# A new order of 375 steps for the opening of a fused retention and two-FFN kernel, with the rows of its loads made 8 KB long

## The chip, the cores and the metric

One core of one Trainium2 chip runs the whole program. The metric is the time of one execution on the device in microseconds (us). A core has five engines that run side by side and meet at semaphores: PE (TensorE, matrix products), DVE (VectorE), ACT (ScalarE), POOL (GpSimd) and SP (SyncE), which here only issues DMAs. 16 DMA engines move data between the HBM and the on-chip memory.

## What is computed

A retention layer (attention with a decay in place of a softmax) on 4 x 8 heads, 576 positions of 64 numbers each, and two feed-forward layers over the 2304 tokens of 512 numbers that come out of it, all in float32:

```python
def _attn_ref(q, k, v):
    scores = scale * np.matmul(q, k.transpose(0, 1, 3, 2))
    Dmat = np.where(rel >= 0, gamma[:, None, None] ** rel[None, :, :], 0.0)
    ret = scores * Dmat[None, :, :, :]
    return np.matmul(ret, v)

def reference(**kwargs):
    x = attn_out.transpose(0, 2, 1, 3).reshape(B * S, H * D)
    x = moe_w_out(leaky(x @ moe_w_in))       # leaky(h) = max(0.01 h, h), 512 -> 2048 -> 512
    h = x @ moe2_w_in                        # 512 -> 2048
    return (h * np.cos(h)) @ moe2_w_out      # 2048 -> 512
```

The inputs w_in and w_out come as 64-bit floats, so the kernel loads their raw words and turns them into float32 itself.

## The kernel before

**Tiles.** The 2304 tokens are cut into 18 chunks of 128 tokens (`ch`, four arrays q, k, k, v of 128 x 512, 1 MB a chunk) and into five blocks of the first feed-forward layer, the first of 512 tokens, which is chunks 0 to 3. The weights of that layer are 16 tiles (f = 0 to 15), each a 1 MB raw tile of 128 x 1024 64-bit words; tiles 0 and 15 are loaded as two halves (`raw0a`, `raw0b`), which belong to w_in and w_out.

**The opening.** All code before the second token block is an order written out by hand, the string `FIRST`: 375 names of steps, played from left to right. Each step puts its instructions on one or more engines, and every engine runs its own instructions strictly in the order in which they were put there. For a chunk i the steps are: `ch` load, `sq` and `sv` scale q and v (DVE; `sv` of some chunks is eight instructions on ACT), `s` scores on PE (16 small matrix products), `m` mask on DVE, `v` values and `g` growth of the state (16 products each), `st.0`, `st.1` state sums on DVE, `r.0` and `r` reads of the state on PE, `tk` the result's move to `xr` on ACT. `xh` and `xl` split that result into a high and a low part (ACT, then DVE). `V` is the whole PE part of a chunk of the second block. For a weight tile f the steps are `raw` load, `abs` and `lo` (ACT), `cs` (two DVE instructions), `or`, `add` (DVE), `hi` (ACT) and `low` (DVE): some 5.5 us of DVE a tile. `H f.k` and `O f` are the products of the first and the second half of the layer with that tile (12 products each), `lk`, `gh` (ACT) and `gl` (DVE) lie between H and O. `~n` are products on constants that nobody reads, n blocks of 128 columns.

**What holds a load back.** All loads go through SP, one after the other. Two of them wait on purpose for PE (`in_turn`): the second half of weight tile 0 and tile 1 wait for the scores of a chunk, tiles 2 and 3 for the growth of chunk 3 (`last_of["grown"]`). What follows in SP's order waits behind them.

**After the opening** a planner's list, `SECOND`, orders the rest: four more token blocks of the first layer, the conversion of the second layer's weights (`mraw`, `more`, in 64 loads of 256 KB), and the second layer. It is the same list in both kernels.

A product of 64 x 64 or 128 x 512 in float32 appears in the trace as two weight loads and two matmuls (four instructions); those of H and O as one of each.

Of the kernel before, what the change touches and what calls it, by code (L numbers as in the profile page):

```python
# [50 lines left out]


FIRST = """
ch0 sq0 s0 sv0 m0 raw0a abs0a cs0a or0a ~3 v0 g0 st0.0 st0.1 ~4 r0.0 ch1 sq1 s1 r0 lo0a add0a ch2 m1 sq2 sv1
hi0a low0a v1 g1 s2 st1.0 st1.1 r1.0 sv2 m2 v2 r1 ch3 sq3 sv3 raw0b raw1 tk0 g2 st2.0 st2.1 s3 m3 abs0b tk1
cs0b or0b lo0b add0b r2.0 r2 v3 g3 st3.0 st3.1 ~5 r3.0 r3 abs1 cs1 or1 lo1 hi0b low0b add1 tk2 tk3 xh0 xl0 xh1
xl1 ch4 sq4 xh2 xl2 xh3 xl3 hi1 low1 raw2 raw3 abs2 cs2 ~13 H0.0 H0.1 H0.2 H0.3 H1.0 H1.1 H1.2 H1.3 lk0 gh0
gl0 lo2 abs3 or2 add2 lk1 gh1 O0 gl1 O1 cs3 hi2 low2 H2.0 H2.1 H2.2 H2.3 sv4 V3 raw4 lo3 or3 add3 abs4 cs4 hi3
low3 raw5 raw7 raw6 raw8 ch5 raw9 raw15a or4 lk2 gh2 gl2 lo4 add4 abs5 cs5 H3.0 H3.1 H3.2 H3.3 O2 hi4 lk3 low4
H4.0 H4.1 H4.2 H4.3 gh3 gl3 O3 lo5 or5 add5 abs6 cs6 hi5 lk4 gh4 low5 H5.0 H5.1 H5.2 H5.3 gl4 O4 lo7 lo6 abs7  # L60
or6 add6 cs7 hi6 low6 lk5 gh5 gl5 or7 add7 H6.0 H6.1 H6.2 H6.3 O5 abs8 cs8 hi7 lk6 low7 H7.0 H7.1 H7.2 gh6 gl6
st4.0 or8 lo8 add8 st4.1 raw10 lo10 sq5 raw11 H7.3 lk7 gh7 gl7 m4 O6 O7 hi8 low8 H8.0 H8.1 abs9 abs10 lo9 sv5
cs9 or9 add9 raw12 cs10 hi9 low9 H8.2 H8.3 V4 ch6 or10 lk8 gh8 st5.0 gl8 st5.1 add10 abs11 cs11 H9.0 H9.1 H9.2
H9.3 lk9 gh9 gl9 O8 O9 or11 tk4 hi10 low10 H10.0 H10.1 H10.2 H10.3 raw15b raw13 lo11 add11 raw14 sv6 sq6 m5 V5
ch7 abs12 hi11 lk10 gh10 cs12 low11 gl10 or12 lo12 add12 lo13 abs13 H11.0 H11.1 H11.2 H11.3 lk11 gh11 hi12 sv7
lo14 cs13 gl11 st6.0 m6 st6.1 sq7 O10 O11 tk5 low12 H12.0 or13 add13 hi13 H12.1 H12.2 H12.3 lk12 gh12 abs14
low13 abs15a gl12 V6 st7.0 st7.1 cs14 or14 H13.0 H13.1 H13.2 H13.3 add14 lk13 gh13 gl13 O12 O13 cs15a hi14
low14 or15a abs15b tk6 lo15b cs15b ch8 H14.0 H14.1 H14.2 H14.3 sq8 sv8 lo15a m7 add15a hi15a low15a V7 st8.0
lk14 gh14 gl14 st8.1 tk7 H15.0 H15.1 H15.2 H15.3 O14 lk15 or15b add15b gh15 gl15 hi15b low15b O15 m8 ch9 sq9
sv9  # L70
"""


# [1534 lines left out]
```

## Time and profile before

| what | value |
|---|---|
| median of 3 runs | 822.32 us (821.81 to 822.36) |
| the profiled execution's own time | 823.17 us |
| its span, first to last instruction | 821.0 us, so 2.2 us lie around it |
| PE busy | 805.4 us (98%) |
| DVE, ACT busy | 645.6 us (79%), 539.5 us (66%) |
| DMA | 203.79 MB, mean 248 GB/s |

The busy shares are means over stages with different limits. The opening, which the change is about, is the first 131 us; in it DVE and PE are both nearly full, and what counts is which of them waits for which, and where.

### The profile page before, as it was taken

Reading aid. Unit: us, or ns where it says so; the run is one execution under the profiler, and the core shown is the slowest. Engines: PE = TensorE matmul, PEld = TensorE weight load, DVE = VectorE, ACT = ScalarE, POOL = GpSimd, SP = SyncE. Lnnn points to the kernel's source line nnn. Section 1 sums busy time; section 2 is a strip of 40 time slices with the busy share of each in tenths; the row PEclk is TensorE's granted clock in tenths of the full one; section 3 lists DMA queues with packets and bytes.
Section 4 is the critical chain, followed back from the end, with each engine's and each line's share of the span. In section 5 each row is a group of like instructions: output and inputs, shape, how many; then the busy total and the mean of one; then the engine's idle time right before and its main releaser. Section 6 shows DMA issues by size and latency. Waiting matters only on the chain.

```text
span 821.0 us, 16054 instructions
## 1 busy us (share of the span) xinstructions
PE 805.4 (98%) x6134; PEld 739.5 (90%) x6134; DVE 645.6 (79%) x1148; ACT 539.5 (66%) x1041; POOL 6.6 (1%) x8
## 2 busy tenths in 40 slices
PE   7899999999999999999999999999999999999997
PEld 4578887888888888999999999999999999999997
DVE  5899988888886868786841278789889788788886
ACT  4788866655655455555542399887868868678761
POOL 0000011000000000000000000000000000000000
PEclk9999999999999999999999999999999999999999
DMA  9774615877878868777579286999748997719544
GB/s 324 274 267 154 231 53 191 263 232 240 270 237 263 261 188 284 243 256 221 193 252 395 109 321 248 338 318 377 279 157 308 306 378 275 261 42 383 199 172 162
DMA packets 101309, 203.79 MB, mean 248 GB/s; under 512 B 9072, under 2 KB 54896, under 8 KB 96112
## 3 DMA queue, kind: packets, MB, share of 16 engines
q1 hardware_dynamic: 101088, 202.41, 70.2%
...
## 4 chain that ended last, share of the span: by engine, by line
PE 82%; DVE 8%; DMA 4%; issue 3%; ACT 2%; SPq 0%; DVEq 0%; POOLq 0%; ACTq 0%
PE psum L1263 21%; PE psum L1435 20%; PE psum L616 19%; PE psum L630 19%; DMA ch<-in_qkv 3%; DMA raw<-in_w 1%; DVE t L569 1%; PE psum L401 1%; DVE t L576 1%; DVE w L588 1%; PE psum L464 1%; PE psum L425 1%; DVE t L560 1%; PE psum L363 1%; DVE acc L1472 0%
## 5 line engine op out<-in xcount | busy, mean ns | idle before, releaser
L616 PE MATMUL psum<-x_sb,w 128*128 128x512 f32 (+1 forms) x960 | 212.4, 370 | 2.7 <-DVE x_sb L852 1.3
L630 PE MATMUL psum<-g,w 128*128 128x512 f32 (+1 forms) x960 | 211.5, 370 | 0.0
L616 PEld LDWEIGHTS psum<-x_sb,w 128*128 128x128 f32 x960 | 174.7, 188 | 28.4 <-DVE x_sb L852 2.2
L630 PEld LDWEIGHTS psum<-g,w 128*128 128x128 f32 x960 | 174.3, 188 | 24.6 <-DVE g L651 1.3
L1263 PE MATMUL psum<-x,ws 128*128 128x384 f32 x576 | 111.2, 334 | 1.0 <-ACT psum L1396 1.0
L1263 PEld LDWEIGHTS psum<-x,ws 128*128 128x128 f32 x576 | 100.7, 188 | 1.5 <-ACT psum L1396 1.4
L917 DVE TENSOR_TENSOR g<-graw,g 128x512 fp32r<-128x512 f32 (+1 forms) x64 | 39.8, 623 | 62.2 <-ACT g L914 62.0
L1263 PE MATMUL psum<-x,wa 128*128 128x384 f32 x432 | 83.9, 334 | 0.0
L1435 PE MATMUL psum<-g,wp 128*128 128x384 f32 x432 | 81.7, 335 | 0.8 <-DVE acc L1472 0.7
L1435 PE MATMUL psum<-g,wq 128*128 128x384 f32 x432 | 80.2, 334 | 0.0
L1435 PEld LDWEIGHTS psum<-g,wp 128*128 128x128 f32 x432 | 75.3, 188 | 1.5 <-DVE acc L1472 1.1
L1263 PEld LDWEIGHTS psum<-x,wa 128*128 128x128 f32 x432 | 75.7, 188 | 0.0
L910 ACT ACTIVATE graw<-psum 128x512 f32<-128x512 f32 (+1 forms) x64 | 34.7, 543 | 62.3 <-PE psum L616 62.2
L1435 PEld LDWEIGHTS psum<-g,wq 128*128 128x128 f32 x432 | 75.4, 188 | 0.0
L914 ACT CAST g<-graw 128x512 fp32r<-128x512 f32 (+1 forms) x64 | 36.3, 567 | 49.5 <-PE psum L630 47.9
L1472 DVE TENSOR_TENSOR acc<-psum,acc 128x384 f32<-128x384 f32 x90 | 48.3, 553 | 18.8 <-PE psum L1435 18.4
L1312 DVE SCALAR_TENSOR_TENSOR r<-r,h 128x768 f32<-128x768 int32 x48 | 45.5, 954 | 6.8 <-ACT r L1307 6.4
L1321 DVE SCALAR_TENSOR_TENSOR h<-r,h 128x768 f32<-128x768 f32 x48 | 45.4, 953 | 5.3 <-ACT r L1318 5.1
L1317 ACT ACTIVATE r<-r 128x768 f32<-128x768 f32 x48 | 40.6, 847 | 9.6 <-DVE r L1312 9.4
L1334 DVE TENSOR_TENSOR g<-tq,g 128x768 fp32r<-128x768 f32 x48 | 45.4, 952 | 1.5 <-ACT g L1338 1.4
L1338 ACT CAST g<-tq 128x768 fp32r<-128x768 f32 x48 | 39.6, 837 | 9.9 <-DVE tq L1355 6.2
L1307 ACT CAST r<-h 128x768 int32<-128x768 f32 x48 | 40.1, 838 | 5.8 <-DVE h L1293 3.6
...
## 6 DMA issues: line engine op xcount, KB each, us to landing
ws<-ws SPq DMA_DIRECT2D x20, 1024.0 KB, 8.2
wp<-wp SPq DMA_DIRECT2D x20, 1024.0 KB, 7.4
ch<-in_qkv SPq DMA_DIRECT2D x17, 1024.0 KB, 6.9
...
raw<-in_w SPq DMA_DIRECT2D x14, 1024.0 KB, 10.4
...
```

The source lines that it names most:

```text
L616: nc.tensor.matmul(hp, wt[:, i, cols], x_t[lj, k][:, j, :n], start=(k == 0 and a == 0), stop=(k == KK - 1 and a == 2),)
L630: nc.tensor.matmul(psum[:, BANK_O + m, :n], wt[:, i, cols], gt[:, j, :n], start=(f == 0 and a == 0), stop=(f == NF - 1 and a == 2),)
L917: nc.vector.tensor_tensor(out=g.ap[:, 1, :n], in0=y.ap[:, :n], in1=g.ap[:, 0, :n].bitcast(F32), op=ALU.subtract)
L1263: nc.tensor.matmul(bank[BANKS[m]].rearrange("p (q t) -> p q t", t=Q), a[:, hl, i, j * P : (j + 1) * P], x[:, :, v, j, :], start=m in (1, 5 ...
L1307: "ACT", 885, lambda: nc.scalar.copy(rb.ap.bitcast(I32), pair()),
L1312: nc.vector.scalar_tensor_tensor(out=rb.ap, in0=rb.ap.bitcast(I32), scalar=-1.0, in1=pair(), op0=ALU.mult, op1=ALU.add)
L1317: t = add("ACT", 885, lambda: nc.scalar.activation(rb.ap, rb.ap, AF.Sin, scale=PI), [t], due)
L1321: nc.vector.scalar_tensor_tensor(out=pair(), in0=rb.ap, scalar=0.5, in1=pair(), op0=ALU.subtract, op1=ALU.mult)
L1334: nc.vector.tensor_tensor(out=gb.ap[:, :, 1], in0=src(), in1=gb.ap[:, :, 0].bitcast(F32), op=ALU.subtract)
L1338: h_ = add("ACT", 885 if n == 2 else 515, lambda: nc.scalar.copy(gb.ap[:, :, 0], src()), [*needs, opened["all"]], due, 0, gb.old)
L1435: nc.tensor.matmul(to, wt[:, hl, i, t * P : (t + 1) * P], gt[:, fi, v, :], start=m in (1, 5) and h == 0 and x == 0, stop=h == 1 and x == 2 ...
L1472: x = add("DVE", 560, lambda: nc.vector.tensor_tensor(out=kept(), in0=to, in1=kept(), op=ALU.add), [got], due - SOON / 2)
```

## The change

It replaces the string `FIRST` by another order of the same 375 steps, moves one gate (the second half of tile 0 and tile 1 now wait for the scores of chunk 2, not of chunk 1), and lays the inputs out in the HBM so that a chunk's or a tile's row in one partition is one piece of 8 KB (4 KB for a half tile) where it was four pieces of 2 KB. The 256 KB loads of the second layer's weights keep pieces of 2 KB, which now lie 8 KB apart and not back to back.

```diff
 FIRST = """
-ch0 sq0 s0 sv0 m0 raw0a abs0a cs0a or0a ~3 v0 g0 st0.0 st0.1 ~4 r0.0 ch1 sq1 s1 r0 lo0a add0a ch2 m1 sq2 sv1
...
+ch0 sq0 s0 sv0 m0 ~1 v0 g0 ch1 sq1 s1 ch2 raw0a st0.0 st0.1 m1 sq2 r0.0 r0 sv1 v1 g1 s2 st1.0 st1.1 m2 r1.0 r1
...
-            got = nc.sync.dma_start(ch, qkv[i].rearrange("x p d -> p x d"))
+            got = nc.sync.dma_start(ch, qkv[i])
...
-        return nc.sync.dma_start(raw.rearrange("p (c t) -> p c t", c=4), w[0, f].rearrange("c p t -> p c t"))
+        return nc.sync.dma_start(raw, w[0, f])
...
             if n == 1 or n == 0 and half:
-                in_turn(got, last_of["scores", 1])
+                in_turn(got, last_of["scores", 2])
...
-                nc.sync.dma_start(rb.ap.bitcast(I64), w[1, f, c])
+                nc.sync.dma_start(rb.ap.bitcast(I64), w[1, f, :, c * 2 * P : (c + 1) * 2 * P])
...
-    arrays = {"in_qkv": np.ascontiguousarray(np.stack(parts, axis=1))}
+    arrays = {"in_qkv": np.ascontiguousarray(np.stack(parts, axis=2))}
...
-        layers.append(np.concatenate([w_in, w_out], axis=2).reshape(NF, P, 4, 2 * P).transpose(0, 2, 1, 3))
+        layers.append(np.concatenate([w_in, w_out], axis=2))
```

The three excerpts below show in which order instructions now stand. The first is SP from the program's start, before (L304, L305 and L307 load chunks, L539 a half tile, L534 a whole tile; PE in the brackets is the gate):

```order
1 L304 DMA ch<-in_qkv 128x2x512
2 L305 DMA ch<-in_qkv 128x2x512
3 L539 DMA raw<-in_w 128x2x256
4 L307 DMA ch<-in_qkv 128x4x512 x3
5 L539 DMA raw<-in_w 128x2x256 [waits PE_49]
6 L534 DMA raw<-in_w 128x4x256 [waits DMAHW0_49]
7 L307 DMA ch<-in_qkv 128x4x512 [waits DMAHW1_49,DMAHW2_49,DVE_49,PE_49]
8 L534 DMA raw<-in_w 128x4x256
9 L534 DMA raw<-in_w 128x4x256 [waits DMAHW3_49]
```

and SP from the start in the changed kernel:

```order
1 L304 DMA ch<-in_qkv 128x1024
2 L305 DMA ch<-in_qkv 128x1024
3 L307 DMA ch<-in_qkv 128x2048 x2
4 L539 DMA raw<-in_w 128x512
5 L307 DMA ch<-in_qkv 128x2048
6 L539 DMA raw<-in_w 128x512 [waits PE_49]
7 L534 DMA raw<-in_w 128x1024 [waits DMAHW0_49]
8 L534 DMA raw<-in_w 128x1024 [waits DMAHW1_49,PE_49]
9 L534 DMA raw<-in_w 128x1024 [waits DMAHW2_49]
```

Chunks 1 and 2 now stand ahead of the first half tile, and behind the growth of chunk 3 come two weight tiles (3, then 2) where chunk 4 came first. Next, PE from the start up to the scores of chunk 2, before (L516 and L522 are products on constants, L363 scores, L401 values, L425 growth, L464 reads):

```order
1 L516 MATMUL psum<-zero 128x512 x3
2 L363 MATMUL psum<-ch 64x64 x16
3 L522 MATMUL psum<-tabs_sb,still 128x384
4 L401 MATMUL psum<-p_sb,ch 64x64 x16
5 L425 MATMUL psum<-ch 64x64 x16
6 L522 MATMUL psum<-tabs_sb,still 128x512
7 L464 MATMUL psum<-ch,st 64x64 x4
8 L363 MATMUL psum<-ch 64x64 x16
9 L464 MATMUL psum<-ch,st 64x64 x4
10 L401 MATMUL psum<-p_sb,ch 64x64 x16
11 L425 MATMUL psum<-ch 64x64 x16
12 L363 MATMUL psum<-ch 64x64 x16
```

and the same stretch of PE in the changed kernel:

```order
1 L516 MATMUL psum<-zero 128x512 x3
2 L363 MATMUL psum<-ch 64x64 x16
3 L522 MATMUL psum<-tabs_sb,still 128x128
4 L401 MATMUL psum<-p_sb,ch 64x64 x16
5 L425 MATMUL psum<-ch 64x64 x16
6 L363 MATMUL psum<-ch 64x64 x16
7 L464 MATMUL psum<-ch,st 64x64 x8
8 L401 MATMUL psum<-p_sb,ch 64x64 x16
9 L425 MATMUL psum<-ch 64x64 x16
10 L363 MATMUL psum<-ch 64x64 x16
```

Before the scores of chunk 2 there stand 109 products before the change and 108 after it. Last, PE from H of tile 2 on, before (L616 is H, L630 is O, w_589 tile 2, w_645 tile 3, w_698 tile 4; L425 and L363 in between are V3, the growth and scores of chunk 4):

```order
30 L616 MATMUL psum<-x_sb,w_589 128x512 x12
31 L425 MATMUL psum<-ch 64x64 x8
32 L363 MATMUL psum<-ch 64x64 x16
33 L616 MATMUL psum<-x_sb,w_645 128x512 x12
34 L630 MATMUL psum<-g,w_589 128x512 x12
35 L616 MATMUL psum<-x_sb,w_698 128x512 x12
```

and there in the changed kernel (L614 is H, L628 O; w_605 is tile 3, w_705 tile 5, w_721 tile 6, w_818 tile 7):

```order
28 L614 MATMUL psum<-x_sb,w_605 128x512 x12
29 L628 MATMUL psum<-g,w_595 128x512 x12
30 L614 MATMUL psum<-x_sb,w_665 128x512 x12
31 L628 MATMUL psum<-g,w_605 128x512 x12
32 L614 MATMUL psum<-x_sb,w_705 128x512 x12
33 L628 MATMUL psum<-g,w_665 128x512 x12
34 L628 MATMUL psum<-g,w_705 128x512 x12
35 L614 MATMUL psum<-x_sb,w_721 128x512 x12
36 L425 MATMUL psum<-ch 64x64 x8
37 L363 MATMUL psum<-ch 64x64 x16
38 L614 MATMUL psum<-x_sb,w_818 128x512 x12
```

V3 has moved from behind H of tile 2 to behind H of tile 6. On DVE the scaling of chunk 4's q (`sq4`) has moved in the same way, from ahead of tile 1's last instruction to behind tile 6's `add`.

## Rows read from the trace of the kernel before

**Rows 1.** The page's chain of work that ended last: shares of the span.

```profile
PE 82%; DVE 8%; DMA 4%; issue 3%; ACT 2%; SPq 0%; DVEq 0%; POOLq 0%; ACTq 0%
```

**Rows 2.** Waits of PE from 48 to 145 us: total, times, longest, us.

```profile
PE psum L616 <- DVE x_sb L852: 1.3, 2, 0.9
```

**Rows 3.** Chain of work that ended last, first 120 us: start, us, what.

```profile
19.43 2.31 issue
...
48.00 2.82 PE psum L616 x11
```

**Rows 4.** DVE in order of time, 17 to 50 us: start, us; brackets: idle before.

```profile
22.49 0.69 DVE L384 TENSOR_TENSOR p_sb<-psum,tabs_sb 128x512 f32<-128x512 f32 x1 [2.15 <-PE psum L363]
23.10 0.42 DVE L560 TENSOR_SCALAR t<-t 128x512 f32<-128x512 f32 x1
...
25.45 0.95 DVE L449 TENSOR_TENSOR st<-psum,st 128x256 f32<-128x256 f32 x2
...
31.84 0.69 DVE L315 TENSOR_TENSOR ch<-ch,tabs_sb 128x512 f32<-128x512 f32 x1
32.44 1.29 DVE L604 TENSOR_TENSOR x_sb<-xr,x_sb 128x512 fp32r<-128x512 f32 x2
...
35.40 0.70 DVE L560 TENSOR_SCALAR t<-t 128x1024 f32<-128x1024 f32 x1 [0.53 <-ACT t L552]
```

**Rows 5.** All engines in order of time, 45 to 137 us.

```profile
46.35 0.51 PE L425 MATMUL psum<-ch 64*64 64x64 f32 x10
...
47.43 3.40 PE L616 MATMUL psum<-x_sb,w 128*128 128x512 f32 x12
...
68.70 1.22 DVE L588 TENSOR_TENSOR w<-t,w 128x1024 fp32r<-128x1024 f32 x1
...
69.92 2.91 PE L616 MATMUL psum<-x_sb,w 128*128 128x512 f32 x12
```

**Rows 6.** Landings, seen by who waits for them, in order of time, 0 to 60 us.

```profile
7.24 0.69 DVE L327 TENSOR_TENSOR ch<-ch,tabs_sb 128x512 f32<-128x512 f32 x1 [0.60 <-DMA ch<-in_qkv]
...
11.35 2.02 ACT L322 ACTIVATE ch<-ch,tabs_sb 128x64 f32<-128x64 f32 x8 [1.50 <-DMA ch<-in_qkv]
...
15.07 0.69 DVE L315 TENSOR_TENSOR ch<-ch,tabs_sb 128x512 f32<-128x512 f32 x1 [1.18 <-DMA ch<-in_qkv]
```

**Rows 7.** Stretches: length, busy by engine (x instructions), clock, DMA share, GB/s.

```profile
40.00:46.00 6.00, 5.95 (x26) 4.54 (x25) 5.83 (x7) 5.48 (x12) 0.00 (x0) 1.00 1.05 385
...
750.00:758.00 8.00, 8.00 (x48) 8.00 (x47) 5.75 (x8) 6.83 (x13) 0.00 (x0) 1.00 1.01 409
```

**Rows 8.** PE in order of time, around three places of the opening.

```profile
15.81 1.13 PE L363 MATMUL psum<-ch 64*64 64x64 f32 x32
...
21.74 0.63 PE L363 MATMUL psum<-ch 64*64 64x64 f32 x27 [2.31 <-issue]
...
25.75 0.49 PE L522 MATMUL psum<-tabs_sb,still 128*128 128x128 f32 x2 [0.29 <-issue]
```

**Rows 9.** Stretches from the start: PE and PEld are the first two (x instructions).

```profile
0.00:19.43 19.43, 15.81 (x348) 9.82 (x348) 10.78 (x21) 8.79 (x26) 0.20 (x4) 0.91 0.93 335
...
0.00:25.70 25.70, 19.36 (x476) 12.25 (x476) 14.59 (x28) 12.91 (x34) 0.20 (x4) 0.93 0.74 262
```

**Rows 10.** Instruction queue, 0.1 us from 12.85, 19.25, 22.85, 31.2: packets, MB, share.

```profile
q8 instruction: 1, 0.02, 70.0%
...
q8 instruction: 1, 0.02, 62.5%
...
q8 instruction: 1, 0.02, 89.7%
...
q8 instruction: 1, 0.02, 54.9%
```

**Rows 11.** One raw tile's load, issued at 62.0 us alone: KB, us to landing.

```profile
raw<-in_w SPq DMA_DIRECT2D x1, 1024.0 KB, 5.0
```

**Rows 12.** The stretch with the low clock, columns as in rows 7.

```profile
14.32:17.73 3.41, 3.08 (x108) 2.71 (x99) 2.56 (x5) 2.66 (x11) 0.00 (x0) 0.50 1.04 372
```

More of the change, by code (lines that the diff above doesn't have):

```diff
@@ L53 @@
 FIRST = """
-ch0 sq0 s0 sv0 m0 raw0a abs0a cs0a or0a ~3 v0 g0 st0.0 st0.1 ~4 r0.0 ch1 sq1 s1 r0 lo0a add0a ch2 m1 sq2 sv1
[L55 to L68, printed above, removed]
@@ L69 @@
-lk14 gh14 gl14 st8.1 tk7 H15.0 H15.1 H15.2 H15.3 O14 lk15 or15b add15b gh15 gl15 hi15b low15b O15 m8 ch9 sq9
-sv9
+ch0 sq0 s0 sv0 m0 ~1 v0 g0 ch1 sq1 s1 ch2 raw0a st0.0 st0.1 m1 sq2 r0.0 r0 sv1 v1 g1 s2 st1.0 st1.1 m2 r1.0 r1
+tk0 abs0a cs0a or0a lo0a add0a ch3 sq3 sv3 sv2 hi0a low0a raw0b raw1 ~8 s3 m3 abs0b cs0b v2 g2 st2.0 st2.1 tk1
+lo0b or0b add0b v3 g3 r2.0 r2 st3.0 st3.1 abs1 lo1 cs1 or1 add1 ~2 r3.0 r3 tk2 tk3 xh0 xl0 xh1 xl1 ~12 H0.0
+H0.1 xh2 xl2 raw3 raw2 raw5 raw4 raw6 raw15a ch4 hi0b low0b xh3 xl3 hi1 low1 abs2 cs2 H0.2 H0.3 H1.0 H1.1 lk0
@@ new lines @@
+gh0 gl0 or2 lo2 abs3 add2 H1.2 H1.3 lk1 gh1 gl1 O0 O1 cs3 hi2 low2 lo3 or3 add3 abs4 cs4 hi3 low3 or4 H2.0
+H2.1 H2.2 H2.3 lk2 ~2 H3.0 H3.1 H3.2 H3.3 gh2 gl2 O2 lo4 add4 raw7 raw8 raw9 ch5 abs5 cs5 hi4 lk3 low4 H4.0
+H4.1 H4.2 H4.3 gh3 gl3 O3 or5 lo5 add5 abs6 lo7 cs6 hi5 low5 or6 lk4 lo6 add6 gh4 gl4 sq4 abs7 raw10 hi6 low6
+H5.0 H5.1 H5.2 H5.3 O4 lk5 gh5 gl5 O5 H6.0 H6.1 H6.2 H6.3 cs7 or7 add7 abs8 cs8 sv4 V3 lo8 hi7 low7 or8 lk6
+gh6 gl6 add8 abs9 cs9 H7.0 H7.1 H7.2 H7.3 raw11 O6 hi8 low8 lk7 gh7 gl7 O7 H8.0 H8.1 H8.2 H8.3 raw15b raw12
@@ new lines @@
+lo9 abs10 or9 add9 lo10 hi9 sv5 sq5 st4.0 st4.1 m4 V4 ch6 low9 cs10 or10 lk8 gh8 add10 m5 gl8 st5.0 abs11 cs11
+H9.0 H9.1 H9.2 H9.3 O8 lk9 gh9 gl9 O9 hi10 low10 st5.1 H10.0 H10.1 H10.2 H10.3 raw13 sq6 or11 lo11 add11 sv6
+abs12 cs12 raw14 tk4 V5 ch7 hi11 lk10 gh10 lo12 low11 abs13 lo13 gl10 or12 add12 hi12 H11.0 H11.1 H11.2 H11.3
+lk11 gh11 st6.0 cs13 st6.1 tk5 sv7 O10 gl11 O11 low12 H12.0 H12.1 H12.2 abs14 or13 m6 add13 hi13 lo15b sq7
+cs14 H12.3 lk12 gh12 low13 abs15a cs15a gl12 or14 lo14 add14 V6 H13.0 H13.1 H13.2 H13.3 lk13 gh13 st7.0 st7.1
@@ L71 @@
+gl13 hi14 m7 O12 O13 ch8 low14 abs15b cs15b or15b tk6 add15b or15a lo15a add15a hi15a low15a H14.0 H14.1 H14.2
+H14.3 hi15b lk14 sq8 sv8 V7 st8.0 st8.1 gh14 gl14 low15b H15.0 H15.1 H15.2 H15.3 O14 lk15 gh15 gl15 tk7 O15 m8
+ch9 sq9 sv9
 """
@@ L303, in load_chunk @@
         if i == 0:
-            nc.sync.dma_start(ch[:, :2], qkv[i, :2].rearrange("x p d -> p x d"))
-            nc.sync.dma_start(ch[:, 2:], qkv[i, 2:].rearrange("x p d -> p x d"))
+            nc.sync.dma_start(ch[:, :2], qkv[i, :, :2])
+            nc.sync.dma_start(ch[:, 2:], qkv[i, :, 2:])
         else:
-            got = nc.sync.dma_start(ch, qkv[i].rearrange("x p d -> p x d"))
+            got = nc.sync.dma_start(ch, qkv[i])
             if i == n_first:
@@ L538, in load_half @@
         raw_t[l, f, s] = raw
-        return nc.sync.dma_start(
-            raw.rearrange("p (c t) -> p c t", c=2), w[l, f, 2 * s : 2 * s + 2].rearrange("c p t -> p c t")
-        )
+        return nc.sync.dma_start(raw, w[l, f, :, s * DM : (s + 1) * DM])
     def words(g):
```

## The prediction

> **What bounds the kernel now.** I read the chain that ended last first: 82% of it is PE, 8% DVE, 4% DMA [rows 1]. So a change of the opening counts by the moment from which PE no longer waits, and by the work that it has done by then. The waits of PE from 48 to 145 us name only 1.3 us, at the border of the first two token blocks, on x splits that stand behind copies of the last O's banks [rows 2]; those copies keep their place in both lists, so this wait stays. Before 48.00 the chain has pieces of everything, with 2.31 us of "issue" among them; from 48.00, H of tile 3 with its weights just there, it is PE without a gap [rows 3]. What holds that H is DVE: it starts the third tile (tile 2) at 35.40, 0.53 us after its last work, and between 22.49 and there it has no other wait [rows 4]. At 22.49 itself it had waited 2.15 us for the scores of chunk 3. So the numbers to move are the start of tile 2 on DVE (35.40) and that of H3 on PE (48.00), and the prediction is made of them.
>
> **Loads.** A stretch of 2 KB pieces runs at 385 GB/s, one with the 6 and 8 KB rows of a later stage at 409 [rows 7]: 1.05 MB in 2.56 us in place of 2.72. Chunk 0's second part had landed by 7.2, chunk 1, behind a half tile, by 11.3, chunk 2 by 15.0 [rows 6]. In the new order chunks 1 and 2 follow directly: 7.2 + 2.6 = 9.8, and 12.4. If the row length gave nothing, they would be 9.9 and 12.6; that difference is hidden under the wait of the next part. On the other side, nothing in these rows makes it more than 6%. Taken alone the landings give chunk 2 some 2.6 us earlier. PE then has scores 1, reads 0, values 1 and growth 1 to do, each about the 0.63 us of the scores in [rows 8], the values behind ACT's 2.0 us of `sv1` [rows 6]: 9.8 + 2.0 + 2 x 0.63 = 13.1, and it is ready for scores 2, where before it began them at 15.81 [rows 8].
>
> **A wait that takes most of it back.** Twice in the opening PE stands still for nothing that the profile names, 2.31 us until 21.74 and 0.29 us until 25.75 [rows 8]. Up to the first stop PE and PEld show 348 + 348 instructions, up to the second 476 + 476: 696 and 952, 256 apart [rows 9]. Around each stop one 16 KB packet moves on the instruction queue; its share of 0.1 us of 16 engines gives its length, 0.700 x 1.6 = 1.12, 1.00 and 1.43 us for the first three [rows 10]. From the second packet's end (19.3 + 1.0) to PE's resumption pass 1.4 us, from the third's (22.9 + 1.4) again 1.4. So PE's code arrives in pieces of 256 instructions, and the piece that starts at instruction 440 is the first packet's: it is there at 12.9 + 1.1 + 1.4 = 15.4. Before, PE came to it at 15.81 and noticed nothing. Now count in the order's excerpt: 108 products stand ahead of scores 2, four instructions each, 432, so the border lies two products into scores 2, where PE is at 13.1. I take the code at 15.4, since the border before it (184, in growth 0) is passed at the same place under the same full DMA traffic. Bounds: 13.1, no wait, and 17.4, with the longest distance from a border to the next packet that I find, 5.5 us (25.75 to 31.2), where that from 15.81 to 19.3 is 3.5.
>
> The Trainium skill, "Runtime: NRT & Kernel Launch", section Instruction fetch mechanics, says that code is refilled in blocks of 16 KiB, 256 instructions, the next while the current one runs, and that crossing a border is mostly hidden. On the size the trace agrees (952 - 696); on the cost it does not, with 2.31 us. By that rule there would be no wait, and the sum would be the first rival's 819.9.
>
> **DVE up to tile 2.** A mask followed PE's resumption by 0.75 us (21.74 to 22.49), so mask 2 starts at 16.2. Behind it DVE has work without a gap: the mask 0.6, the four steps of half tile 0a 2.35 (as 23.10 to 25.45), `sq3`, `sv3` and `low0a` at 0.6 each (as `sq4`, 31.84 to 32.44) [rows 4]: mask 3 at 20.9. From mask 3 to tile 2 it was 22.49 to 35.40 less the idle 0.53, 12.4 us; `sq4` leaves it (-0.6), the states of chunk 2 come in (+0.95, as the two at 25.45): 12.7. Tile 2 starts at 33.7, 1.7 us earlier than 35.40. What covers this: the second half of tile 0 and tile 1 are now asked for behind scores 2, at about 16.1, on an empty queue, where a whole tile takes 5.0 us [rows 11]: about 20 and 22.5 for the two, and DVE, past ACT's `abs`, needs them at 21.5 and 25. With that cover gone each us later would cost one. Growth 3 ends at about 22.7; tiles 3 and 2 behind it land by 27.7 and 30.2, and DVE needs tile 2, past ACT, by 32.5. With chunk 4 still ahead of them it would be 32.8, a new wait.
>
> **From tile 2 to the full PE.** The steps of tiles 2 and 3 keep their order, so H3 starts at 48.0 - 1.7 = 46.3. But PE has then done less: V3, 1.08 us (46.35 to 47.43), which lay ahead of H3 where PE waited anyway, now stands between H6 and H7, where PE is full [rows 5]. From H3 to H7 it was 69.92 - 48.00 = 21.9; with V3 it is 23.0: H7 at 69.3, 0.6 us ahead of before. DVE, with `sq4` now in this stretch, ends tile 7 at 69.92 - 1.7 + 0.6 = 68.8, early enough by 0.5. Its `gl` for O7 comes behind five instructions (1.2 + 0.6 + 1.2 + 1.4 + 1.2) and takes 0.7: 75.1, where PE is ready at 69.3 + 5.5 = 74.8: 0.3 us lost. Then PE is full to the end of the token block, and what follows is the same list. The pieces of the second layer's 256 KB loads lie 8 KB apart now; I price this at nothing, since PE's waits show no DMA there [rows 2], and as the bound on the other side at the 0.3 us by which one late conversion could hold an H.
>
> **Sum:** -1.7 + 1.1 + 0.3 = -0.3. On the profiled execution's 823.17 (span 821.0 + 2.2 around it) that is 822.9; on the median of the runs, 822.32, which lies 0.85 lower, **822.0 us**. Its own range, with 0.5 us either way on each of the two DVE stretches, is 821.0 to 823.0. A measurement of this kernel tells about 0.2% from no change, 1.6 us.
>
> **Rivals.**
> - *The code is there in time.* Scores 2 run at 13.1 and mask 2 comes 2.3 us sooner; chunk 3's landing, by 16, and mask 3 behind it give 0.2 back. Tile 2 starts at 31.6, and PE ends 2.4 us ahead: 819.9. For it: the fetch may come out of the queue sooner when a DMA has fewer, longer pieces. Against it: the borders and packets of [rows 8 to 10].
> - *The code comes later,* the slower end. With 5.5 us from border to packet it is there at 17.4; mask 2, the gate on scores 2 and all behind them move by 2.0: 824.0. The sign turns with the code at 15.7, 0.3 us later than I take it; from 17.3 on it is slower by more than 0.2%. For it: the packet at 31.2, under loads as dense as these. Against it: the 3.5 us under the same chunk loads.
> - *PE at half clock.* From 14.32 to 17.73 the granted clock was 0.50, the 1.2 GHz level [rows 12]. The same there now would lengthen scores 2 by some 0.4 us (1.13 at 15.81 against 0.63 to 0.7 [rows 8]): 822.4, within the first case's range.
> - *DVE falls behind in the second half of the opening.* DVE and PE run level there: tile 7 ends at 68.70 + 1.22 = 69.92, when H7 starts [rows 5]. Each further wait like O7's costs 0.3 to 0.7; three make 823.5.
>
> **How the numbers follow.** The sum as above, half clock included: 0.56. Code in time: 0.27. Code later: 0.11. DVE behind: 0.06. Faster by over 0.2% are the second case and the lucky edge of the first, 0.29; slower the third and half of the fourth, 0.14; within it 0.57. The range reaches down to the second case's 819.9 and up to most of the third: 819.8 to 823.8.
>
> **What would show it.** In the changed kernel: an unnamed wait of PE of about 2.3 us inside scores 2, ending near 15.4, with the instruction queue's packet near 12.9; DVE's first instruction on the third tile near 33.7 and H3 near 46.3; V3 behind H6 with PE full around it; a wait of 0.3 us ahead of O7. If scores 2 run through before 14, or that wait ends past 17, one of the first two rivals holds and the sum is off by about 2 us. It is wrong as well if DVE waits for a raw tile between 20 and 34 us, or if PE has new waits between 70 and 131 us.

## The result, and the profile after

The changed kernel takes 828.01 us (median of 6 runs, 825.06 to 830.04), the kernel before beside it 822.33 (6 runs, 821.71 to 822.75): ratio 1.0068, 95% interval 1.0053 to 1.0083. On another chip it was 1.0049 (1.0032 to 1.0066, 9 runs). So it is slower by 4 to 6 us, where I had forecast 822.0 and a range up to 823.8. Its runs also spread more here, 5 us in place of 1; in larger samples on other chips the kernel before spread by 3 to 6 us too. The profiled execution took 827.15 us, with a span of 825.3, 4.3 more than before. The page of the changed kernel, its span, and the chain that ended last by engine:

```profile
span 825.3 us, 16058 instructions
...
PE 78%; DVE 8%; DMA 5%; issue 4%; ACT 4%; SPq 0%; DVEq 0%; ACTq 0%; POOLq 0%
```

PE's share of the chain fell from 82% [rows 1], and DMA, issue and ACT gained: the chain has waits in it that were not there. PE of the changed kernel in order of time, at the places where it waited and at the stations of the forecast (brackets: idle before, and what ended it; the changed kernel's lines stand two lower than before's from about L534 on):

```profile
16.72 0.91 PE L363 MATMUL psum<-ch 64*64 64x64 f32 x26 [2.49 <-issue]
...
47.44 0.49 PE L614 MATMUL psum<-x_sb,w 128*128 128x512 f32 x1 [0.26 <-ACT graw L639]
...
70.48 0.51 PE L425 MATMUL psum<-ch 64*64 64x64 f32 x10
...
71.56 3.02 PE L614 MATMUL psum<-x_sb,w 128*128 128x512 f32 x12
...
97.15 0.69 PE L401 MATMUL psum<-p_sb,ch 64*64 64x64 f32 x32 [1.35 <-ACT xr L503]
...
105.42 3.06 PE L628 MATMUL psum<-g,w 128*128 128x512 f32 x12 [0.50 <-DVE g L649]
...
127.63 3.04 PE L614 MATMUL psum<-x_sb,w 128*128 128x512 f32 x12 [1.20 <-ACT graw L639]
...
136.13 8.66 PE L614 MATMUL psum<-x_sb,w 128*128 128x512 f32 x36
...
147.43 2.96 PE L614 MATMUL psum<-x_sb,w 128*128 128x512 f32 x12
...
209.53 3.06 PE L614 MATMUL psum<-x_sb,w 128*128 128x512 f32 x12 [0.51 <-ACT graw L908]
```

The code wait in scores 2 is there, as forecast, but it ends at 16.72 and not at 15.4. V3 stands in full PE from 70.48. H7 starts at 71.56, 1.64 us later than before [rows 5], where I had it 0.6 earlier. Then come three waits that sum to 3.05 us, and at 136.13 none at the block border, where before had 1.3 [rows 2]. The next H behind an O, at 147.43, answers to this row of the kernel before, same view:

```profile
144.32 2.94 PE L616 MATMUL psum<-x_sb,w 128*128 128x512 f32 x12
```

That is 3.11 later. The spans end 4.3 apart, so the last 1.2 us were lost behind 147, in small waits such as the one at 209.53. Three places, then, in this execution: before H7, from H7 to the border, and in the rest, whose code and list are the same. A second profile of the same kernel (`after_again`, below) shares the first and the last; from H7 to that H it has waits of 1.06 us and not 3.05. The first place begins with the first loads, as DVE of the changed kernel shows:

```profile
6.87 0.69 DVE L315 TENSOR_TENSOR ch<-ch,tabs_sb 128x512 f32<-128x512 f32 x1 [5.34 <-DMA tabs_sb<-in_tabs]
...
17.78 0.69 DVE L384 TENSOR_TENSOR p_sb<-psum,tabs_sb 128x512 f32<-128x512 f32 x1 [2.66 <-PE psum L363]
...
22.55 0.68 DVE L384 TENSOR_TENSOR p_sb<-psum,tabs_sb 128x512 f32<-128x512 f32 x1
...
35.42 0.68 DVE L558 TENSOR_SCALAR t<-t 128x1024 f32<-128x1024 f32 x1
```

DVE's first instruction, the scaling of chunk 0, waits for the tables (`tabs_sb`, the load on ACT's queue) until 6.87; before it started at 5.95. Mask 2 at 17.78, mask 3 at 22.55 and tile 2 at 35.42 are all 1.6 to 1.7 us behind the forecast's 16.2, 20.9 and 33.7. Chunk 0's first part itself had landed at 6.68, where before it landed at 5.85.

### The profile page after: what moved, and what is told of

The parts are those of the page before. It is cut to its first block, busy times and chain, and to the rows that moved or that the text cites. A ratio compares the mean times of both kernels' runs of the same rounds, so it can differ in the third digit from the quotient of the medians.

```text
span 825.3 us, 16058 instructions
## 1 busy us (share of the span) xinstructions
PE 805.9 (98%) x6134; PEld 739.1 (90%) x6134; DVE 644.2 (78%) x1148; ACT 540.7 (66%) x1041; POOL 5.8 (1%) x8
## 4 chain that ended last, share of the span: by engine, by line
PE 78%; DVE 8%; DMA 5%; issue 4%; ACT 4%; SPq 0%; DVEq 0%; ACTq 0%; POOLq 0%
PE psum L1261 21%; PE psum L1433 20%; PE psum L628 18%; PE psum L614 17%; DMA ch<-in_qkv 3%; DVE t L574 1%; DVE t L567 1%; DMA mraw<-in_w 1%; DVE w L586 1%; PE psum L401 1%; PE psum L464 1%; PE psum L425 1%; PE psum L363 1%; DMA raw<-in_w 1%; DVE t L558 1%
## 5 line engine op out<-in xcount | busy, mean ns | idle before, releaser
L614 PE MATMUL psum<-x_sb,w 128*128 128x512 f32 (+1 forms) x960 | 212.5, 370 | 2.9 <-ACT graw L639 1.5
L628 PE MATMUL psum<-g,w 128*128 128x512 f32 (+1 forms) x960 | 211.6, 370 | 0.8 <-DVE g L649 0.5
L614 PEld LDWEIGHTS psum<-x_sb,w 128*128 128x128 f32 x960 | 174.6, 188 | 29.5 <-DVE x_sb L602 2.0
L628 PEld LDWEIGHTS psum<-g,w 128*128 128x128 f32 x960 | 174.4, 188 | 25.8 <-DVE g L649 1.7
L1336 ACT CAST g<-tq 128x768 fp32r<-128x768 f32 x48 | 39.6, 838 | 10.1 <-DVE tq L1353 6.4
```

The lines of the kernel that those rows point to most:

```text
L614: nc.tensor.matmul(hp, wt[:, i, cols], x_t[lj, k][:, j, :n], start=(k == 0 and a == 0), stop=(k == KK - 1 and a == 2),)
L628: nc.tensor.matmul(psum[:, BANK_O + m, :n], wt[:, i, cols], gt[:, j, :n], start=(f == 0 and a == 0), stop=(f == NF - 1 and a == 2),)
L1336: h_ = add("ACT", 885 if n == 2 else 515, lambda: nc.scalar.copy(gb.ap[:, :, 0], src()), [*needs, opened["all"]], due, 0, gb.old)
```

## The experiments

All ratios are to the kernel before on the same chip. "To H" is the start of the H that is at 144.32 before; "rest" is the span less that; "first" is DVE's first instruction on chunk 0, "code" the end of the first wait for code (new list only; it lies in scores 2, with the list of `s2_early` in growth 1), "load" the page's median landing of the second layer's `mraw` loads.

| run | ratio (95%) | first | code | to H | rest | load |
|---|---|---|---|---|---|---|
| before | 1 | 5.95 | | 144.3 | 676.7 | 3.9 |
| changed | 1.0068 (53 to 83) | 6.87 | 16.7 | 147.4 | 677.9 | 4.2 |
| after_again | 1.0049 (32 to 66) | 6.78 | 16.7 | 146.3 | 679.4 | 4.2 |
| rows_only | 1.0028 (16 to 40) | 6.87 | | 145.6 | 679.9 | 4.1 |
| list_only | 1.0011 (1 to 20) | 5.49 | 15.2 | 145.2 | 676.0 | 3.7 |
| tk4_first | 1.0063 (50 to 75) | 6.73 | 16.6 | 148.5 | 676.9 | 4.4 |
| s2_early | 1.0040 (27 to 54) | 6.75 | 16.4 | 146.8 | 678.8 | 4.4 |
| old_chunks | 1.0031 (19 to 44) | 5.80 | 15.2 | 144.7 | 676.7 | 4.1 |
| old_raw | 1.0031 (18 to 44) | 6.48 | 16.4 | 146.4 | 679.7 | 4.3 |
| old_pitch | 1.0033 (20 to 46) | 6.70 | 16.8 | 147.3 | 676.5 | 3.3 |
| pitch_only | 1.0017 (4 to 30) | 5.50 | | 142.8 | 678.1 | 4.2 |
| first_chunk | 1.0026 (9 to 43) | 5.60 | 16.0 | 144.6 | 679.8 | 4.4 |
| hybrid | 1.0001 (-12 to 14) | 5.44 | 15.4 | 145.5 | 676.2 | 3.8 |
| hybrid_old_list | 0.9990 (-23 to 3) | 5.54 | | 143.1 | 676.7 | 3.5 |
| ch0_halves | 1.0045 (29 to 62) | 5.53 | 14.6 | 145.0 | 677.7 | 4.2 |
| tabs_first | 1.0025 (12 to 38) | 6.77 | 16.4 | 144.7 | 677.2 | 4.1 |
| hybrid_s2 | 1.0013 (3 to 23) | 5.91 | 15.9 | 144.9 | 676.0 | 3.4 |
| hybrid_old_list2 | 1.0009 (-2 to 19) | 5.55 | | 142.7 | 677.3 | 3.4 |
| padded | 1.0015 (0 to 29) | 5.70 | 15.8 | 146.3 | 677.5 | 3.9 |

(Intervals in units of 0.0001 above 1.) The single profiles scatter by a microsecond or two, so the columns are read in groups.

**Rows or list.** The theory: the list did it, by the code wait and by steps that stand wrongly in its second half. The rival: the rows did it. Two kernels split the change:

```diff
 rows_only: the changed kernel with the old FIRST and
-                in_turn(got, last_of["scores", 2])
+                in_turn(got, last_of["scores", 1])
 list_only: the kernel before with the new FIRST and
-                in_turn(got, last_of["scores", 1])
+                in_turn(got, last_of["scores", 2])
```

> The old list of steps and its gate on scores 1, with the new host layout (rows of 8 KB, second-layer loads with a pitch of 8 KB). If the layout costs nothing, as I priced it: ratio 1.000 (822.3 us), first chunk landed by 5.9 as before. If the rows themselves delay the first landings and the instruction queue (the changed kernel has its first chunk 0.83 us later, at 6.68, and the first code packet at 14.18 in place of 12.89): first chunk near 6.7, and 0.8 to 1.5 us more, 1.001 to 1.002. If the second layer's loads are hurt by the pitch, new waits of PE for converted second-layer weights behind 137 us, about 1 us in all.

> The new list with its gate on scores 2, in the old layout (rows of 2 KB). If the list is the whole cause: ratio 1.005 to 1.008, the unnamed wait of PE in scores 2 ending past 16 us, a wait of 1.3 us ahead of the reads of chunk 5 (near 96 us) and one of 1.2 near 126. If the rows of 8 KB made the code late: scores 2 resume near 15.4 to 15.9, everything behind 0.8 to 1.3 us earlier, 1.003 to 1.005.

The list alone costs 0.9 us of 822, the rows alone 2.3, together 3.2 of the 4.0 to 5.6 of the whole change: the rival holds, for the larger part. In `rows_only` both signs are there, the first instruction at 6.87 and a rest of 679.9. In `list_only` DVE and then a stretch of the whole core (columns as in [rows 7]) read:

```profile
5.49 0.69 DVE L314 TENSOR_TENSOR ch<-ch,tabs_sb 128x512 f32<-128x512 f32 x1 [3.96 <-DMA ch<-in_qkv]
...
16.36 0.69 DVE L383 TENSOR_TENSOR p_sb<-psum,tabs_sb 128x512 f32<-128x512 f32 x1 [2.26 <-PE psum L362]
...
22.36 0.69 DVE L383 TENSOR_TENSOR p_sb<-psum,tabs_sb 128x512 f32<-128x512 f32 x1 [1.14 <-PE psum L362]
...
35.00 0.69 DVE L559 TENSOR_SCALAR t<-t 128x1024 f32<-128x1024 f32 x1
```

```profile
17.50:21.30 3.80, 3.80 (x14) 1.22 (x8) 3.54 (x6) 1.98 (x6) 0.00 (x0) 0.50 0.74 238
```

The first scaling is at 5.49 and mask 2 at 16.36, where the forecast had 16.2. Mask 3 then waits 1.14 us for PE, which from 17.5 to 21.3 runs the fill of 8 blocks at the granted clock of 0.50, the 1.2 GHz level, behind its code wait. So tile 2 gains 0.4 us and not 1.7. How long PE stays at that level differs between executions. In the changed kernel the clock is 0.50 from 16.9 to 20.3, behind the code wait too. In `after_again`, the same kernel, it is 0.50 from 9.7 to 23.3, so it had fallen ahead of the code wait, and mask 3 waits 1.06. In `old_chunks`, with the same list, it is 1.00 from 15 to 26, and mask 3 does not wait. So the 1.14 is not a fixed price of the list.

**One step of the second half.** tk4 stands behind sv6 in the new list, and ACT is at sv6 when chunk 6 lands (92.4). The diff is one name of `FIRST`:

```diff
-... raw13 sq6 or11 lo11 add11 sv6 abs12 cs12 raw14 tk4 V5 ...
+... raw13 tk4 sq6 or11 lo11 add11 sv6 abs12 cs12 raw14 V5 ...
```

> The changed kernel with one step moved: tk4 (ACT copies the read-outs of chunk 4 out of their banks) ahead of sq6 and sv6, which wait for chunk 6. If PE's 1.35 us wait near 96 us comes of ACT standing at sv6 until chunk 6 has landed (92.4): that wait is gone, the 0.5 and 1.2 us waits behind it shrink too, and the time falls by 1.3 to 3 us to 825.0 to 826.7 (1.003 to 1.005). If DVE's own work is what is late there: the same 3 us of waits move to the next O and H, and the time stays within 0.5 us of the changed kernel's 828.0 (1.007).

The wait at 97.15 is gone, the time stays (1.0063): PE of `tk4_first` waits for other work of ACT and DVE, in the same sum:

```profile
98.30 0.49 PE L613 MATMUL psum<-x_sb,w 128*128 128x512 f32 x1 [0.87 <-ACT graw L638]
99.46 4.36 PE L613 MATMUL psum<-x_sb,w 128*128 128x512 f32 x11 [0.66 <-DVE w L585]
...
128.79 3.04 PE L613 MATMUL psum<-x_sb,w 128*128 128x512 f32 x12 [1.57 <-ACT graw L638]
```

0.87 + 0.66 + 1.57 = 3.10 us, against 3.05. (From 100.3 to 103.7, behind the second of these waits, its granted clock is 0.50.) But the changed kernel, with `tk4` where it was, has no wait at that place in its second profile, `after_again`, where chunk 6 landed at 91.28 and not at 92.41:

```profile
104.78 3.02 PE L628 MATMUL psum<-g,w 128*128 128x512 f32 x12 [0.31 <-DVE g L649]
...
126.55 3.04 PE L614 MATMUL psum<-x_sb,w 128*128 128x512 f32 x12 [0.75 <-ACT graw L639]
```

So that it is gone in one profile shows little; that the time stays is what counts. My theory of that step falls. That ACT and DVE are what PE waits for there is read off the waits; why they are late is not tested.

**Scores 2 ahead of the border of the code.**

```diff
-... sv1 v1 g1 s2 st1.0 st1.1 m2 r1.0 r1 tk0 abs0a cs0a or0a lo0a add0a ch3 ... raw1 ~8 s3
+... sv1 s2 m2 v1 g1 abs0a cs0a or0a lo0a st1.0 st1.1 r1.0 r1 tk0 add0a ch3 ... raw1 ~3 s3
```

> The changed kernel with scores 2 and mask 2 ahead of values 1 and growth 1, the states of chunk 1 behind the steps of half tile 0a on DVE, and the fill behind it cut from 8 to 3. PE then has scores 2 before the border of its code pieces, and the border falls into growth 1. If the code wait at scores 2 is what held DVE from 15.1 to 17.8: mask 2 near 14.9, the gate of the second half tile open by 14.5 and that half tile landed near 18.5, tile 2 started on DVE 2 to 2.7 us earlier (near 33 in place of 35.4), and 825.3 to 826 us if the second half of the opening keeps its 3 us of waits (1.004 to 1.005). If DVE waits somewhere else instead: tile 2 past 35 and 828 (1.007).

Mask 2 came at 14.9, the gate opened, and tile 2 still started at 35.57: mask 3 now waited for scores 3. The 1.0040 looks like a gain, but repeated in a better layout (`hybrid_s2`, below) the same list was 1.0013, and the new list unchanged 1.0001, with intervals that overlap. The code wait moved into growth 1, and no gain can be told from noise. In this profile PE ran at a granted clock of 0.50 from 13.6 to 23.8, scores 3 with it.

**Which rows.** The expectations call the distance from one piece to the next the pitch. Three kernels put one part back in its old layout, a fourth changes one part alone in the kernel before:

```diff
 old_chunks: chunks only
-    arrays = {"in_qkv": np.ascontiguousarray(np.stack(parts, axis=2))}
+    arrays = {"in_qkv": np.ascontiguousarray(np.stack(parts, axis=1))}
 old_pitch: second layer only (old_raw: first layer only, in the same way)
-                nc.sync.dma_start(rb.ap.bitcast(I64), w[1, f, :, c * 2 * P : (c + 1) * 2 * P])
+                nc.sync.dma_start(rb.ap.bitcast(I64), w[1, f, c * P // 4 : (c + 1) * P // 4].rearrange("a (b t) -> (a b) t", t=2 * P))
 pitch_only: old list and gate, old chunks, old first layer
```

> The changed kernel with the chunks of q, k and v alone back in the old layout (rows of 2 KB); weights as changed. In the two profiles with 2 KB rows the tables on ACT's queue had landed at 4.5 and 5.0 us and chunk 0's first part at 5.4 and 5.8; in the four with 8 KB rows at 6.7 to 6.8 and 6.6 to 6.7. If it is the chunks' rows that hold the tables and the first chunk back: landed by 5.0 and 5.9 again, the first code wait ends near 15.3 to 15.7, and 1 to 2 us less than the changed kernel: 826 to 827 us, 1.004 to 1.006. If not: first landings as in the changed kernel and 828 (1.007).

> The changed kernel with the first layer's weights alone back in the old layout (2 KB pieces). If the first layer's rows of 8 KB are no loss, as their rate says (2.50 us apart in place of 2.70): the time stays at 828 or rises by up to 0.5 us, 1.006 to 1.008. If they cost by holding other queues or landings back (code packets, the chunk behind them): 1 us or more less, below 1.0055.

> The changed kernel with the second layer's 256 KB loads alone back in one contiguous piece each. Their mean time to landing was 3.8 us in the two profiles with contiguous pieces and 4.2 to 4.4 in the four with the pitch. If that pitch costs, by conversions on ACT that wait longer: landings at 3.8 again, the waits of PE behind 137 us gone, and 1 to 3 us less: 825 to 827, 1.003 to 1.0055, with a smaller spread of the runs. If I priced it rightly at nothing: 828, 1.006 to 1.0075.

> The kernel before with the second layer's loads alone changed (2 KB pieces, 8 KB apart); list, chunks and first layer as before. If the pitch costs by itself: 0.8 to 2 us more than before, 1.001 to 1.0025, with landings at 4.2 and waits of PE behind 137 us. If it only delays in company with the other rows: 1.000, within 0.0007.

Each of the three gave some 3 us back, more together than there was to give, so the changed kernel was timed again, beside the next three. The traces are clearer than the times: `old_chunks` has its first instruction at 5.80 and 144.7 to H; `old_pitch` has loads of 3.3 us and a rest of 676.5; `pitch_only` has neither the late start nor a late H, and 678.1 of rest. `old_raw` has both faults of the changed kernel (6.48, 679.7), but its profiled execution, 827.92, is the slowest of its eight (median 824.52). Its 1.0031 stays unexplained, and I take no share for the first layer's rows.

**The two parts that are left.** Chunk 0 alone, and chunk 0 with the second layer, back in the old layout, with either list:

```diff
 first_chunk: chunk 0 in pieces of 2 KB, stored back to back
+    arrays["in_qkv"][0] = np.stack([p[0] for p in parts]).reshape(P, 4, DM)
-            nc.sync.dma_start(ch[:, :2], qkv[i, :, :2])
+            nc.sync.dma_start(ch[:, :2], qkv[i, : P // 2].rearrange("(x a) y d -> (a y) x d", x=2))
 hybrid: first_chunk with old_pitch
 hybrid_old_list: hybrid with the old list and gate
```

> The changed kernel once more, on another chip and beside the three below. The single parts back in their old layout gave 1.0031 to 1.0033 each, the list alone 1.0011, all three rows with the old list 1.0028: sums of these make 1.005 to 1.006 for the changed kernel. If the 1.0068 of its first runs holds here too, the rows cost more together than apart; if it is 1.004 to 1.0055, the parts add up and part of the 1.0068 was that chip.

> The changed kernel with chunk 0 alone stored as before (2 KB pieces); all other chunks and weights in rows of 8 KB. If it is chunk 0's 4 KB pieces that hold back the tables on the other queue: tables landed by 5.0 and chunk 0's first part by 5.9, as with all chunks old, and 2 to 3 us less than the changed kernel (1.003 to 1.004). If the long rows behind chunk 0 do it: tables past 6 us, and the changed kernel's time.

> The new list with chunk 0 in 2 KB pieces, the other chunks and the first layer in rows of 8 KB, the second layer's loads contiguous. If chunk 0's pieces and the pitch are the two costs of the layout: 822.0 to 823.1 us, ratio 0.9995 to 1.001, no slower than the new list in the old layout (1.0011), since the loads behind are 0.2 us per MB faster. If rows of 8 KB cost elsewhere: 1.002 or more.

> The same layout with the old list and gate. If the two costs are all that the layout has: 0.999 to 1.000, and the difference to the run before it is the list's own price, 0.5 to 1 us. If the rows of 8 KB cost elsewhere: above 1.001.

On one chip: 1.0049, 1.0026, 1.0001, 0.9990. Of the changed kernel's 4.0 us there, chunk 0 makes 1.9, the second layer's loads 2.1, the list 0.9, and the other 8 KB rows take off 0.8 at most: all single intervals overlap their neighbours', but the traces show the same three. All runs of the new list in groups (the list of `s2_early` left out) say it more loosely: with a late chunk 0 and second-layer loads 8 KB apart the mean ratio is 1.0047 (the changed kernel twice, `tk4_first`, `old_raw`, `tabs_first`), with those loads alone 1.0034 (`old_chunks`, `first_chunk`, `ch0_halves`), with the late chunk 0 alone 1.0033 (`old_pitch`), with neither 1.0009 (`list_only`, `hybrid`, `padded`). So each of the two is worth some 1 to 2 us, my estimate from these means. In the column "to H" the six profiles of these with a late first instruction have 146.8 in the mean, the six others 145.2. The start, stretches of the changed kernel and then of `first_chunk` (columns as in [rows 7]):

```profile
3.00:4.00 1.00, 1.00 (x2) 0.34 (x1) 0.00 (x0) 0.00 (x0) 0.00 (x0) 1.00 0.95 274
4.00:5.00 1.00, 1.00 (x2) 0.34 (x1) 0.00 (x0) 0.00 (x0) 0.00 (x0) 1.00 1.00 293
```

```profile
3.00:4.00 1.00, 1.00 (x2) 0.34 (x1) 0.00 (x0) 0.00 (x0) 0.00 (x0) 1.00 1.00 364
4.00:5.00 1.00, 1.00 (x2) 0.34 (x1) 0.00 (x0) 0.00 (x0) 0.00 (x0) 1.00 1.04 398
```

The DMA engines are as busy (0.95 and 1.00), and move 274 and 293 GB/s in place of 364 and 398. And the second layer, first DMA issues of `after_again` from 137 to 400 us, then of `hybrid` (KB, median us to landing):

```profile
more<-in_w SPq DMA_DIRECT2D x31, 256.0 KB, 4.2
mraw<-in_w SPq DMA_DIRECT2D x30, 256.0 KB, 4.1
```

```profile
mraw<-in_w SPq DMA_DIRECT2D x30, 256.0 KB, 3.6
more<-in_w SPq DMA_DIRECT2D x30, 256.0 KB, 3.5
```

Who pays is seen in ACT's waits, in `rows_only` and then in `hybrid` over the same list, 137 to 420 us (total, times, longest):

```profile
ACT mraw L1136 <- DMA mraw<-in_w: 15.3, 9, 3.6
ACT mraw L1134 <- DMA mraw<-in_w: 12.2, 6, 4.3
ACT more L1134 <- DMA mraw<-in_w: 11.8, 5, 3.7
```

```profile
ACT more L1135 <- DMA mraw<-in_w: 8.3, 4, 3.1
...
ACT mraw L1135 <- DMA mraw<-in_w: 6.0, 5, 3.3
ACT mraw L1137 <- DMA mraw<-in_w: 4.7, 4, 2.0
```

ACT stands 39.3 us for these loads where it stood 19.0. The two are near the ends of what the profiles show: 18.9 to 22.8 in the seven with contiguous loads, 21.8 to 39.6 in the eleven with loads 8 KB apart, 19.0 in `padded`. Most of it is slack; what is not comes back as PE's wait for the copies that ACT does behind them, as at 209.53, in some places and in some executions: the rest is 676.0 to 677.3 in the seven profiles with contiguous loads and 676.7 to 679.9 in the eleven with loads 8 KB apart, 1.9 more in the mean. The difference lies ahead of the second layer's first product: from H to there it is 319.6 to 320.8 us in the seven, 320.3 to 323.3 in the eleven, 319.6 in `padded`.

The 1.9 is somewhat too high, because the eleven profiled executions happen to lie 0.6 us above the medians of their kernels, and the seven 0.05: `rows_only`, the largest rest, is its kernel's slowest run. That leaves some 1.4 us, and 1.4 (0.3 to 2.5) is what `pitch_only` costs. The spread of the runs goes the same way, with standard deviations of 1.1 to 2.2 us in the eleven kernels and 0.6 to 1.3 in the six contiguous ones other than before; but `padded` spreads by 1.7 without the late loads, so the cause of the spread is not shown.

**Why chunk 0 is late.** Theory: the size of its pieces, which beside the tables' queue take a larger share. Rival: the 8 KB from one piece to the next.

```diff
 ch0_halves: two contiguous halves, pieces of 4 KB
+    halves = [np.stack([p[0] for p in parts[x : x + 2]], axis=1) for x in (0, 2)]
+    arrays["in_qkv"][0] = np.stack(halves).reshape(P, 4, DM)
 tabs_first: the tables ahead of chunk 0 on SP's queue
-        nc.scalar.dma_start(tabs_sb, tabs)
+        nc.sync.dma_start(tabs_sb, tabs)
 padded: every row padded to 12 KB
+    np.pad(np.stack(parts, axis=2), ((0, 0), (0, 0), (0, 2), (0, 0)))
+    np.pad(np.stack(layers).view(np.int64), ((0, 0), (0, 0), (0, 0), (0, DM)))
```

> The changed kernel with chunk 0 stored as two contiguous halves: its two loads still have pieces of 4 KB, but the pieces follow each other without a gap instead of lying 8 KB apart. If the size of the pieces holds the tables back (packets of the two queues taken turn by turn, so that a longer packet takes a larger share): tables past 6.3 us and chunk 0's first part past 6.2, as in the changed kernel (6.5 to 6.9 and 6.3 to 6.7), and 1.004 to 1.007. If it is the 8 KB between the pieces: tables by 5.2, chunk 0 by 5.9, and the 1.0026 of the run with chunk 0 in its old layout.

> The changed kernel with the tables' load on SP's queue ahead of chunk 0 in place of ACT's queue; all rows as changed. If the two queues share the engines by packets: alone, the tables land by 3.9 to 4.5, chunk 0's first part by 5.7 to 6.3 behind them, DVE starts up to 0.9 us earlier than at 6.87, and the time falls by 0.5 to 1.5 us to 1.002 to 1.005. If the 4 KB pieces are slow by themselves: chunk 0's first part still at 6.5 or later, and the changed kernel's time (1.005 to 1.007).

> The changed kernel with every row in the HBM padded from 8 to 12 KB, so that the pieces of chunk 0 (4 KB) and of the second layer's loads (2 KB) lie 12 KB apart in place of 8, and the 8 KB rows of the other loads have gaps of 4 KB. If it is the distance of 8 KB, a power of two, that makes them slow: tables by 5.6, chunk 0's first part by 5.5, second-layer loads landed in 3.3 to 3.9 us (median), and 1.000 to 1.002. If any gap between the pieces costs: tables past 6.3, chunk 0 past 6.2, 4.0 us or more, and the changed kernel's 1.005 or above, since the whole rows have gaps now too.

DVE's first instruction in these three, in this order:

```profile
5.53 0.69 DVE L315 TENSOR_TENSOR ch<-ch,tabs_sb 128x512 f32<-128x512 f32 x1 [4.00 <-DMA tabs_sb<-in_tabs]
```

```profile
6.77 0.69 DVE L315 TENSOR_TENSOR ch<-ch,tabs_sb 128x512 f32<-128x512 f32 x1 [5.23 <-DMA ch<-in_qkv]
```

```profile
5.70 0.69 DVE L315 TENSOR_TENSOR ch<-ch,tabs_sb 128x512 f32<-128x512 f32 x1 [4.16 <-DMA tabs_sb<-in_tabs]
```

Pieces of 4 KB without a gap start DVE at 5.53, and from 3 to 5 us the DMA engines move 374 and 415 GB/s: not the size. With the tables out of the way (landed at 3.90), the gapped pieces still land at 6.67, at 279 GB/s from 4 to 5 us: not the sharing. With 12 KB from piece to piece, 5.70 (333 and 416 GB/s), and `padded` has its second-layer loads at 3.9 us too:

```profile
more<-in_w SPq DMA_DIRECT2D x31, 256.0 KB, 3.5
mraw<-in_w SPq DMA_DIRECT2D x30, 256.0 KB, 3.9
```

So it is the distance of 8 KB; only 8 and 12 KB were tried, and why 8 KB is slow is not shown. The times follow with less certainty. `padded` is 1.0015, 2.8 to 4.4 us better than the changed kernel with the same list and pieces. `ch0_halves` is 1.0045 though its start is early, and `tabs_first` 1.0025 though its start is late: there H7 comes at 71.0 and the stretch to H takes 73.7 us, where the changed kernel needs 75.9 from 71.56. That is not the tables' doing: the changed kernel itself needs 73.8 from 72.53 in `after_again`. Why the second half of the opening takes 2 us more in one execution than in another is not settled.

**Two more lists in the better layout.**

> The mixed layout (chunk 0 in 2 KB pieces, second layer contiguous) with the new list in which scores 2 and mask 2 stand ahead of values 1 and growth 1, and the fill behind is 3 in place of 8. In the changed kernel's layout this list was 1.004 against 1.005 to 1.007. If the new list loses by the code wait in scores 2 and the fills: 1 to 2 us below the mixed layout's 1.0001, 0.9975 to 0.999, below the old list's 0.999. If DVE has no use for the earlier mask: 1.000.

> The old list in the mixed layout once more, since its 0.999 (0.9977 to 1.0003) did not tell it from the kernel before. If the 8 KB rows of the later chunks and of the first layer give their 0.2 us per MB: 0.9985 to 0.9995 again; if that was chance: 1.000.

`hybrid_s2` (mixed layout, list of `s2_early`) shows on DVE that the early mask brings nothing:

```profile
13.98 0.69 DVE L383 TENSOR_TENSOR p_sb<-psum,tabs_sb 128x512 f32<-128x512 f32 x1 [1.17 <-PE psum L362]
...
22.20 0.69 DVE L383 TENSOR_TENSOR p_sb<-psum,tabs_sb 128x512 f32<-128x512 f32 x1 [1.93 <-PE psum L362]
```

Mask 2 is 2.2 us ahead of `hybrid`'s 16.14, and mask 3 waits 1.93 for scores 3, which PE runs in 1.13 us:

```profile
21.00 1.13 PE L362 MATMUL psum<-ch 64*64 64x64 f32 x32
```

In `hybrid` it is 0.69 us from 20.33. The granted clock in `hybrid_s2` is 0.50 from 13.0 to 23.2, as in the profile of `s2_early`, and in `hybrid` only from 16.3 to 19.7. What the early mask would bring at the full clock is not shown. `hybrid_old_list2` is 1.0009 after 0.9990: the 8 KB rows of the other loads give nothing that can be measured. No version beats the kernel before.

## Why the prediction was wrong, step by step

- **What bounds the kernel**: right in part. The start of the full PE and V3 count, but the waits behind it eat most of what it gains: in `ch0_halves` and `old_chunks` H7 starts at 69.55 and 69.83, nearly where I had it (69.3), and the H behind the border still comes at 145.0 and 144.7, after waits of 2.6 and 1.8 us.
- **Loads**: the step that failed. "Chunk 0's second part had landed by 7.2" was taken from the old layout, and row length was weighed by the rate of long streams [rows 7] alone; "nothing in these rows makes it more than 6%". In the stream that holds: tiles land 2.50 us apart in place of 2.70. The first load of the program is not in a stream, and its pieces lie 8 KB apart: 274 GB/s where packed ones move 364, the first instruction at 6.87 and chunk 1 at 10.5 where I had 9.8. My sum had nothing for this; the runs make it 1.9 us, from `after_again` to `first_chunk`. From this come later masks, and in part the later code: PE passes instruction 184 at 10.20 and not at 9.46. In part only, since `first_chunk` passes it at 9.1 and its code is there at 16.02: the next packet comes 3.2 to 4.7 us behind that border, where I had taken 3.5.
- **The second layer's loads**, "I price this at nothing", bound 0.3: this failed too, by 1.4 us (`pitch_only`) to 2.1 (`first_chunk` to `hybrid`). I looked only at PE's named waits for a DMA [rows 2]; the wait was ACT's, and reached PE as a wait for ACT.
- **The code wait**: right in mechanism, 1.2 to 3.0 us in scores 2, and with the old layout right in time (it ends at 15.21, forecast 15.4). The rival by which it is hidden did not happen. *The code comes later* did, half way: 16.72 is 1.3 us later than 15.4, which by that rival's own reckoning (2.0 us for 17.4) gives 823.3, and 828.0 was measured.
- **DVE up to tile 2**: the working held where its inputs did. `hybrid` has masks at 16.14 and 21.09 and tile 2 at 34.20, `ch0_halves` 33.41, against 16.2, 20.9, 33.7. *PE at half clock* I had put at 0.4 us in scores 2; it sat in the fill behind, cost mask 3 1.14 in `list_only`, and lasted 3.4 us in one execution of the changed kernel and 13.6 in another, which no term of mine allowed for.
- **V3, +1.1**: right: from 70.48 to 71.56 it is PE's own time.
- **O7, +0.3, and "then PE is full to the end of the token block"**: wrong. In `list_only` PE waits 0.30 at 103.4 and 1.00 at 125.4, in the changed kernel 3.05 us in one profile and 1.06 in the other, and the 1.3 of the border, which I said would stay, goes. That 1.3 was one execution's: three of the five profiles with the old list have no such wait. This is the rival *DVE falls behind*, with a chance of 0.06; moving the one step `tk4` did not remove it.
- **The sum for the list**, -0.3: measured +0.9 (0.1 to 1.6), by `list_only`. With chunk 0 and the second layer, which the sum had at nothing, that makes up the 4.0 us of `after_again`. The 1.6 us more of the first six runs have no cause here, and the two intervals overlap.

A page of the Trainium skill, "Perfetto Trace Analysis", section DMA Optimizations, advises pieces of 4 or 8 KB over 2 KB. For the long streams here the trace agrees (2.50 us per MB against 2.70); for chunk 0 it does not, since the larger pieces came with a distance between them, and DVE's first instruction on it starts 0.9 us later.
